# A new listed order of all steps in a fused attention and MLP kernel

## The chip, the cores and the metric

The kernel runs on one core of a Trainium2 chip. A core has five engines, each with an instruction stream of its own: TensorE (PE in the profile, with PEld for its weight loads), VectorE (DVE), ScalarE (ACT), GpSimd (POOL) and SyncE (SP), which here only starts DMA transfers. The metric is the device time of one execution in microseconds (us); lower is better.

## The reference

Two blocks follow each other. The first is a cross attention between 512 tokens and 32 states for each of 8 batches and 8 heads of width 64, in both directions. The second is an MLP on the 8 x (512 + 32) = 4352 rows that come out, with `d_model` 512 and `d_ff` 2048. All of it is float32; the two weights arrive as 64-bit floats.

```python
scores  = x @ state.T / 8;   a  = softmax(scores)    # (B, H, 512, 32)
xread   = a @ state
scores2 = state @ x.T / 8;   a2 = softmax(scores2)   # (B, H, 32, 512)
sread   = a2 @ x
rows    = concat(xread, sread)      # (B*544, H*64) after a transpose of heads
h       = rows @ w_in
out     = (h * erf(softplus(h))) @ w_out             # (4352, 512)
```

## The kernel before

**The order.** Every piece of work is a named step: `step(name, f)` (L248) stores a function, and nothing is issued when the steps are defined. At the end of the kernel (L1156 to L1164) a loop walks through `ORDER`, a list of 2532 names that fills lines 23 to 179, and issues each step in its turn through `issue` (L182). `in_order` (L1149) then fixes that every engine carries out its instructions in exactly this sequence. So each engine has a strict queue of its own, cut out of the one list: a step that has to wait holds up all that stands behind it on its engine, while the other engines go on until they need something from it. Semaphores for the data and for the reuse of buffers are put in by the framework from what each step reads and writes. Of the steps, 749 run on PE, 743 on DVE, 684 on ACT, 100 on POOL and 256 on SP.

```python
    for name in ORDER.split() or do:
        if name[0] == "~":
            k, n = name[1:].split("*")
            issue(name, lambda: warm(bank[int(k)][:, 0:P], int(n)))
        else:
            issue(name, do.pop(name) if ORDER.split() else do[name])
    in_order(begun)
```

A name such as `~7*3` is a filler: `warm` (L429) issues 3 products of the identity matrix into bank 7, which nobody reads. A float32 product shows up as two matmul instructions, a transpose as one.

**The start.** `load_x0` (steps `lx0` to `lx3`, L340) brings batch 0 of x, half of it on ACT's queue and half on SP's; `load_raw` (`i0l0`, `o0l0`, ...) brings the weights. `convert` (L375) turns 64-bit words into float32 in four steps: `a0` and `a1` on ACT, a shift `v0` on DVE (L383), and an integer add `v1` (L385), which for the first eight pieces (`i0` to `i3`, `o0` to `o3`, `BY_GPSIMD`, L20) runs on GpSimd and for the others on DVE. Piece `i0` comes in two parts (`i0...` and `i0+...`).

`attention0` (L433) handles batch 0. `x00` to `x31` turn x into banks (`xik`, with copies `xikc`; L444), `s0` turns the states (copies `s0c0`, `s0c1`, `s0c`), `t0` and `t1` are the token scores, `q0` and `q1` the state scores (copies `q0c`, `q1c`). For each half of the tokens, `max`, `less`, `exp`, `sum`, `inv` and `norm` make the softmax, `ta0` and `ta1` transpose it and `ta0c`, `ta1c` copy it to `y[0]`. The state softmax follows in `rest` (`big0`, `big1`, `big`, `wt`, `wz`, `wn`, transposes `tw0`, `tw1` with copies), then `read(0)` (L528): the product `rd0`, its copy `rn0`, a transpose `rt0`, a copy `rc0`. `ub` turns the states of batch 1.

`first_unit` (L967) is the MLP of batch 0. `n01`, `n00`, `n02`, `n10`, `n12` multiply states with parts of `w_in` (copies `...c0` on ACT and `...c1` on DVE), so that h can be had straight from the softmax; `h0L`, `h0R` to `h7L`, `h7R` (L987) are its half products, with a softplus `hks` (ACT), a copy `hkc` (DVE), an erf `hke` and a product `hkg`. The products with `w_out` are `o00` to `o36` (L1009), copied by `o0c` to `o3c` and stored by `o0d` to `o3d`.

**The units after it.** Batches 1 to 7 go through `attention(b)` (L554): loads `a1xq0` to `a1xq7` on SP, transposes `a1tx` on DVE, the scores `a1s` on PE, copies `a1c0`, `a1c1`, and two softmaxes. `load_st` (`lst1` to `lst8`, L363) brings their states on GpSimd's queue; `hold` is a one-column copy on GpSimd. Unit A1 to A7 is the first half of `d_ff` for a batch, SA and SB are the rows of the states, B0 to B7 the second half of `d_ff`. Within a unit, `mixed` (L646; `A1m`, `A1M1` to `A1M4`) multiplies states with `w_in`; `hidden` (L695, products L704) makes h with a scheme of seven products instead of eight block products, laid out by `chain` (L669): products `A1f01` to `A1f07` and `A1f11` to `A1f17` accumulate into three PSUM banks, with copies `c`, `u2`, `c11`, `u3`, `c21` (ACT) and adds `c22`, `c12` (DVE) between them, then softplus `s..`, erf `A1e0`, `A1e1` (L712) and products `A1g0`, `A1g1`. A copy from a bank to the next bank or to SBUF must be done before the next product may accumulate there.

`second_twice` and `inner` (L767 to L882) do the product with `w_out` by the same scheme at two levels, on products of 128 columns (L827): `A1ap10`, `A1ap11`, ... for the first four of the seven outer products, `A1bp...` for the other three, with copies `ac`, `au2`, `ac11`, `au3`, `ac21` (ACT) and adds `ac22`, `ac12` (DVE). `A1a2` to `A1a4` and `A1b2` to `A1b4` are sums of the left operands, `U2`, `U3`, `U4`, `C2`, `C12` sums of results in the buffer `res`, and `d0` to `d3`, `D0`, ... the stores (L735): plain ones on SP, accumulating ones on POOL. `res` is reused by the next unit, so `B2au2`, which writes it, waits for the store of unit B1 that reads the same part. In the second half of the kernel `second_last` (L884) is the last unit, B7, with adds `B7v..` and `B7C120`, `B7C121` and stores by halves, down to `B7d11`.

**Lists of weights.** `twice` (`t..`, `w..`) and `restore` prepare and take back the sums of `w_out` for the two-level scheme; `y11` to `y14` and the like (`sums_y`, L624) are sums of the softmax rows, kept in DRAM by `yk..`, `yl..` on SP until the second half loads them again (`yK..`, `yL..`).

Of the kernel before, what the change touches and what calls it, by code (L numbers as in the profile page):

```python
# [40 lines left out]
a3xq7 a2mx0 A1f1s12 o06 a3xq3 a2my0 a2sb0 A1e0 o14 a3xq1 a2x3 t32 A1e1 A1g0 t0k o16 a3xq6 A2m
a3xq5 A1g1 a2ex0 yk0 t1k o26 o0c t2k A2m11 a2x2 a2sm0 t4k A2m10 a2ey0 o30 a2iz a3tx0 a2x0 o1c
a2nm0 t6k A2m01 o2c a3tx2 o32 t3k a2ey1 A2m00 A2M1 a2ta0 o34 t42 y21 A2f01 a2ty0 a2ty1 o36 A2f0c
y22 a2kz A2M2 o2d t21 A2f06 y23 o3c t22 A2M3 A2f02 A2f0u2 A1q A2f05 A2f0c11 t23 A2f07 y24 A1A1
A1ap50 A2f0u3 A2f11 t44 a2z2 t12 o3d A2f0c22 A2f04 a2z1 t13 a2z0 A1ap10 A1A3 a2z3 A2f0c21 yk2
A2f1c A1ap11 yl2 A2M4 o0d A2f12 A1A2 A2f16 A2f0s22 T3 A2f03 A2f1u2 t62 A2f0s11 t5k A1ap51 t51 yk1
a2iy t02 A2f17 o1d t03 t33 t34 rd2 A2f1u3 A1A4 A1ac A2f14 rn20 t04 a3x0 rn21 A2f1c11 A2f0c12 rt2
A1ap20 A1a2 rc2 a3s A1b2 A1ap60 A1a3 a3c0 a4xq5 a3c1 A1ap61 a4xq6 t24 a3tu0 A1ap21 A1au2 a4xq3
A2f0s12 A2f15 t53 A1ac11 a4xq2 a3mx0 A1ap70 A2f0s21 a4xq1 A2f1c22 A1ap71 a3sb0 a3my0 a4xq0 A1bp10
A1au3 a3x3 A1ac22 A1bp11 A2f13 t14 t52 a3ey0 A1ap40 A1b4+ A1a4 a3ex0 A1ap41 t43 a3ey1 A1ap30 a3sm0  # L50
A1ac21 A1ap31 A1bc a3iz A2f1c21 A2f1c12 a3nm0 A1bp60 A1ac12 A1bp61 a4tx0 A1d0 A3m A2f1s12 a4xq7
A2f1s22 t54 A2f1s21 a3ta0 a4xq4 A1bu2 A1bp50 A3m00 A1b3 A2f1s11 A1bp51 A3m11 y31 A3f01 a3ty0 A3m01
A1bp20 A3m10 a3ty1 A1D0 A3f0c a3iy A1bp21 t63 a3kz A3M1 A1bp70 a3x2 t64 A1d2 y32 A1bp71 A2e0 A3M2
A3f05 A1b4 A3f06 A3M3 A1bu3 A3f02 y34 A3f0u2 y33 A1bc22 A2e1 A1bp40 a4tx2 A3f07 a3z3 A2g0 a3x1
A1bp41 A1bc11 a3z2 A1bp30 A3f0u3 a3z1 A3f0c11 a3z0 A3f04 A1bc21 A3f0c22 A3f11 A2g1 A3f0c21 A1bp31
A3f1c A2ap10 A3f16 A3M4 A3f12 A3f1u2 A1bc12 A2q A3f03 A1d1 A1d3 rd3 yl3 A3f0c12 A2A1 A3f17 rn30
a4x2 rn31 rt3 A2A3 A2ap50 rc3 A3f1u3 A3f15 A2A2 A3f14 A1D1 A3f1c22 A3f0s21 A2ap11 A3f0s11 A2A4 a4s
A2ac A2a2 A3f1s22 A2ap20 A3f1c21 a5xq1 A1U2 A3f1s12 A2ap60 A2a3 a5xq2 a4c1 A2ap61 a4c0 yk3 A1U3
a5xq3 A3f13 A2b2 A2au2 A1D4 A2ap21 A3f0s12 a4tu0 A3f1c11 A2ap70 a5xq7 A3f0s22 A2b4+ A2ac11 a4mx0
A2ap71 a5xq0 A3f1s11 A2ap51 A3f1c12 A2au3 a4sb0 a4my0 A2bp10 A3f1s21 A2bp11 A2ac22 A2ap40 a4x0  # L60
A1D2 A2a4 a4ex0 A2ap41 A1D3 A2b4 A2ap30 A2ac21 a4sm0 a5xq5 A2bc A2ap31 a4ey0 a4iz A2bp60 a4ey1
A2ac12 a4nm0 a5tx0 A2bp61 A4m A3e0 a4ta0 A2bp20 A4m11 A2b3 a4x1 A2bp21 A4m01 A2bp50 a4x3 a4ty0
A2bu2 A4m10 A2bp51 a4ty1 A4m00 A2bp70 y41 a4kz A3e1 A4M1 a5xq4 A2bp71 y43 A4f01 A4M3 a5xq6 A4M2
A4f05 A2bu3 A4f0c y42 A2d0 A2bp40 A2bc22 A2d2 A3g0 A4f06 A2bp41 A4f0u2 A4f02 A2bc11 a4iy a4z3 y44
A4f07 A3g1 a4z2 a4z0 A2bp30 A4f0u3 a4z1 A4f0c11 A2bp31 A2bc21 A4f04 A2D0 A4f0c22 A4f11 A2bc12
A4f0c21 A4M4 A2d1 A3ap10 A4f1c A3q A2d3 A4f03 a5tx2 A4f16 rd4 A2U2 A4f1u2 A3A1 A4f17 rn40 a5x0
rn41 A4f0c12 rt4 A3ap11 A2D1 A4f1u3 A3A2 rc4 A4f14 yl4 A3A3 A4f15 A4f0s22 A2U3 a5s A3a2 A2D2 A4f12
a5c0 a6xq0 A3A4 A3ac A3ap50 a5c1 a6xq2 A4f0s21 A3ap20 A4f1c22 A2D4 A3b2 A4f1c21 A3ap60 A4f1s22
a5tu0 A3ap61 A4f13 A3a3 A3au2 a6xq1 A4f0s12 A3ap21 a5mx0 A4f1c11 a5x1 A3ap70 A4f1s12 a6xq3 A3ac11
a5my0 a5sb0 A3ap71 a6xq7 A4f1c12 A3ap51 A3au3 A3bp10 A3ac22 A2D3 A3a4 A3ap40 a5ex0 A3bp11 A3b3  # L70
a5ey0 A3ap41 a6xq5 a5ey1 a5sm0 A3ap30 a6xq6 A3ac21 A3ap31 yk4 a5iz a5nm0 A5m A4f0s11 a6tx0 A3bc
A4f1s11 A3ac12 A3bp60 A5m01 a5ta0 A3d0 A5m10 A3bp61 A3d2 A5m11 A3bp20 a5ty0 A3bu2 A4f1s21 A3bp21
y51 a5ty1 A5m00 A3bp70 A5M1 a5kz A3bp71 a5iy A3d3 A5f01 y52 A5M3 A4e1 A3bp50 A3b4+ A3b4 A3D0
A3bp51 A5M2 A5f05 A3bu3 y53 A5f0c A3bc22 A3bp40 A4e0 y54 A4g1 A5f06 A3bp41 a5z0 A5f0u2 A5f02 a5x2
a5z1 A5M4 A5f07 a5z3 A5f0c11 A4g0 a5z2 A3bc11 A3bp30 a5x3 A5f0u3 A3bp31 a6xq4 A5f04 A5f0c22 A5f11
A3bc12 A5f0c21 A4q A5f03 A5f1c A3bc21 A4ap10 A3U2 A3d1 A5f16 yk5 A4A1 yl5 A5f12 A5f1u2 A5f0c12 rd5
A4A3 A5f17 rn51 a6tx2 rn50 A5f1c11 A4ap11 A5f1u3 A4A2 A3D1 rt5 A5f14 rc5 A4ac A3U3 a6s A4a2 A3D2
A5f15 a6c1 a7xq0 A4a3 a6c0 A4ap60 a7xq5 a6tu0 A4ap50 A5f1s11 A4ap61 A5f0s11 a6mx0 A4ap20 A4au2
A5f1c22 A5f0s12 a6sb0 A4ap21 a6my0 A5f1s22 a7xq4 A4ap70 A4ac11 A4ap51 A4A4 A3D4 A4ap71 a6ex0 A3D3
A4b2 A4bp10 A4au3 a6sm0 a6ey1 A4bp11 a7xq7 A5f13 a6ey0 a6iz A4ap40 A5f1c21 A5f1c12 a6nm0 A4ac22  # L80
A4ap41 A6m A5f0s21 A4ac21 A4a4 A4bc a6x2 A5f1s12 a6ta0 a7xq3 A4bp20 A6m00 A5f0s22 a7xq2 A4bp60
A4b3 A6m10 A6m11 A4bp61 a6ty1 A4ap30 A6m01 a7xq6 y61 A5f1s21 A6M1 A4ap31 A4bu2 a7xq1 a6ty0 A4bp21
# [1112 lines left out]
```

## Time and profile before

| what | value |
|---|---|
| median of three runs | 681.45 us (681.26, 681.45, 682.07) |
| span of the profiled execution | 680.2 us, 1.25 below the median |
| mean granted TensorE clock | 1.00 |
| instructions | 13851 |
| products of the two-level scheme (L827) | 47% of the chain that ended last |
| products of `hidden` (L704) | 27% of that chain |
| DMA | 87.15 MB, mean 128 GB/s |
| first x data lands | 4.19 us |
| PE never idle from / to | 36.36 / 676.4 us |
| last store lands | 678.91 us |

The span is the time from the first to the last recorded event of the profiled execution; the runs were timed without the profile. "Busy" is the time in which an engine had at least one instruction under way. The clock is the share of full speed that TensorE was granted. The chain that ended last is found by going back from the last instruction, at each step to what released it.

Starts of some steps in the profiled execution, in us: `t0` 8.34, `ta0` 15.12, `ta1` 17.34, `h1L` 17.83, `n02` 19.65, `n10` 23.41, `n12` 27.33, `rd0` 31.54, `a1s` 35.10, `A1m` 41.66, `A1f01` 48.79, `A1f06` 51.74. Twelve of the sixteen half products `h..` start before `a1s`.

### The profile page before, as it was taken

What the parts mean: (1) busy time and instruction counts of PE and PEld (TensorE: products, weight loads), DVE (VectorE), ACT (ScalarE), POOL (GpSimd) and SP (SyncE); (2) the same over time, 40 slices, a digit from 0 to 9 for tenths busy, and PEclk for the clock granted to TensorE, in tenths of its full rate; (3) what the DMA queues carried; (4) which work ended last, traced back from release to release, by engine and by line L of the source; (5) the groups of instructions that cost most, each with busy time, mean ns of one, the idle gap of its engine ahead of it and who ended that gap; (6) DMA issues with size and microseconds to landing.
All of it is one profiled execution on the core that took longest, in us unless ns stands there. A gap on an engine that the chain in (4) does not pass through costs nothing.

```text
span 680.2 us, 13851 instructions
## 1 busy us (share of the span) xinstructions
PE 673.4 (99%) x5584; PEld 590.2 (87%) x5584; DVE 581.1 (85%) x760; ACT 485.4 (71%) x759; POOL 130.9 (19%) x106
## 2 busy tenths in 40 slices
...
GB/s 299 219 249 118 198 219 98 163 163 191 159 185 158 145 173 123 156 139 136 224 271 212 58 63 115 72 61 57 32 83 34 44 29 116 19 67 18 46 89 121
DMA packets 145839, 87.15 MB, mean 128 GB/s; under 512 B 92784, under 2 KB 138096, under 8 KB 145776
## 3 DMA queue, kind: packets, MB, share of 16 engines
...
q10 hardware_dynamic: 544, 0.52, 0.2%
...
## 4 chain that ended last, share of the span: by engine, by line
PE 96%; DMA 1%; DVE 1%; SPq 1%; issue 0%; DVEq 0%
PE b L827 47%; PE b L704 27%; PE b L655 4%; PE b L1009 4%; PE b L1049 4%; PE b L757 4%; PE b L925 2%; PE b L987 1%; DMA big<-in_x_dram 1%; PE b L564 1%; PE b L539 1%; SPq L354 1%; PE b L456 1%; PE b L444 0%; DVE ring L244 0%; PE b L976 0%
## 5 line engine op out<-in xcount | busy, mean ns | idle before, releaser
L735 POOL DMA_DIRECT2D out_dram<-res x67 | 80.1, 1422 | 424.8 <-DVE res L242 205.9
L827 PEld LDWEIGHTS b<-big,ring 128*128 128x128 f32 x1196 | 145.4, 192 | 6.9 <-issue 1.7
L827 PE MATMUL b<-big,ring 128*128 128x128 f32 x1196 | 151.1, 275 | 0.0
L250 ACT COPY ring<-b 128x512 f32<-128x512 f32 (+1 forms) x136 | 78.4, 585 | 92.9 <-PE b L704 76.3
L704 PE MATMUL b<-y,m 128*128 128x256 f32 x480 | 121.3, 381 | 0.0
L250 ACT COPY res<-b 128x512 f32<-128x512 f32 (+2 forms) x126 | 64.6, 522 | 51.7 <-PE b L827 37.9
L704 PEld LDWEIGHTS b<-y,m 128*128 128x128 f32 x480 | 86.6, 190 | 12.3 <-issue 1.9
L704 PE MATMUL b<-sy,m 128*128 128x256 f32 x360 | 91.4, 381 | 0.0
L244 DVE TENSOR_TENSOR ring<-ring 128x2048 f32<-128x2048 f32 (+1 forms) x36 | 78.1, 2172 | 8.7 <-ACT ring L712 8.2
L693 ACT ACTIVATE ring<-ring 128x512 f32<-128x512 f32 x128 | 77.9, 632 | 2.5 <-DVE ring L242 2.0
L242 DVE TENSOR_TENSOR ring<-ring,b 128x512 f32<-128x512 f32 (+1 forms) x72 | 47.2, 658 | 31.3 <-PE b L704 15.2
L827 PEld LDWEIGHTS b<-ta,ring 128*128 128x128 f32 x548 | 67.7, 192 | 7.2 <-issue 3.4
L704 PEld LDWEIGHTS b<-sy,m 128*128 128x128 f32 x360 | 64.8, 190 | 10.0 <-issue 2.6
L827 PE MATMUL b<-ta,ring 128*128 128x128 f32 x548 | 72.4, 276 | 0.0
L243 DVE TENSOR_TENSOR ring<-ring 128x1024 f32<-128x1024 f32 (+3 forms) x66 | 70.7, 1080 | 0.1
L827 PE MATMUL b<-big,ta 128*128 128x128 f32 x572 | 70.7, 275 | 0.0
L827 PEld LDWEIGHTS b<-big,ta 128*128 128x128 f32 x572 | 67.8, 192 | 1.3 <-ACT b L250 0.8
L242 DVE TENSOR_TENSOR res<-res,b 128x512 f32<-128x512 f32 (+2 forms) x60 | 36.2, 604 | 27.4 <-PE b L827 15.6
L712 ACT ACTIVATE ring<-ring 128x2048 f32<-128x2048 f32 x30 | 57.2, 1913 | 0.2
L250 ACT COPY b<-b 128x512 f32<-128x512 f32 (+2 forms) x63 | 34.3, 547 | 16.1 <-PE b L704 8.2
L242 DVE TENSOR_TENSOR res<-res 128x512 f32<-128x512 f32 (+1 forms) x56 | 42.1, 753 | 2.3 <-ACT res L250 1.3
L242 DVE TENSOR_TENSOR ring<-ring 128x1024 f32<-128x1024 f32 (+1 forms) x35 | 39.8, 1143 | 0.3
...
## 6 DMA issues: line engine op xcount, KB each, us to landing
...
```

The source lines that it names most:

```text
L242: add = lambda o, a, b: tt(o, a, b, op=ALU.add)
L243: sub = lambda o, a, b: tt(o, a, b, op=ALU.subtract)
L244: mul = lambda o, a, b: tt(o, a, b, op=ALU.mult)
L250: do[name] = lambda: f(*args)
L655: pe.matmul(out=to[j][e][q, :], lhsT=by, rhs=w_in[r, 4 * j:4 * j + 4, i, :], start=True, stop=True)
L693: act.activation(out=o, in_=i, func=ACTF.Softplus)
L704: pe.matmul(out=to[:, i], lhsT=xs[n - 1][:, q:q + P], rhs=ys[n - 1], start=(start and i == 0), stop=(i == 1), skip_group_check=True)
L712: step(u + "e%d" % o, lambda s=s: act.activation(out=s, in_=s, func=ACTF.Erf))
L735: nc.gpsimd.dma_start(out=to, in_=of, accum_op=ALU.add)
L757: pe.matmul(out=to[:, E2 * h:E2 * h + E2], lhsT=a[:, k // 2, k % 2], rhs=rhs[n][:, k], start=(start and h == 0 and k == 0), stop=(k == 3), ...
L827: pe.matmul(out=out_[:, P * j:P * j + P], lhsT=lhs[:, i], rhs=rhs[:, i], start=(start and j == 0 and i == 0), stop=(i == 1), skip_group_ch ...
L1009: pe.matmul(out=bank[3 + r % 3], lhsT=s[:, k, P * r:P * r + P], rhs=wo[0].w[:, k, :], start=(k == 0), stop=(k == NT - 1))
```

## The change

Only the list `ORDER` is different. The new list has the same 2532 names, the three fillers `~7*3`, `~7*1` and `~7*5` included, each once; no step's function, buffer or engine is touched, and what depends on what stays the same. The order of all steps is another, from the first line to the last. In the start, for example:

- `~7*3` stands ahead of `x30` (before: behind `exp1`), `~7*1` behind `x20`, and `x20`, `x00` ahead of `x10`;
- `q0` and `q1` stand ahead of `t1`;
- `h1L` stands ahead of `ta1`, and `n02` ahead of `ta1` and `h0L`;
- `i0v1` stands ahead of `i0+v1`, `norm1` behind `i1v1`, `o0a1` behind `h1s`, `h0s` and `n12c0`;
- the loads `lst1` to `lst8` are spread over the start (before: all behind `hold`);
- more of the products `o..` stand ahead of `A1f06`.

Later, `B1C2` and `B2au2` stand nearer to each other, and in the last unit `B7D0` stands ahead of the stores of `B6`, and the adds `B7v..` and `B7C120`, `B7C121` have another sequence on DVE; PE's last steps keep theirs. The diff has 155 lines on each side; the places named here are these:

```diff
@@ -21,161 +21,161 @@
-warm lx3 own lx2 lst0 lx1 lx0 i0l0 i0l1 i1l0 i1l1 i2l1 x30 s0 x30c x10 s0c0 s0c1 x31 x10c x20 x00
-x20c x11 i2l0 x00c x21 x01 i0a0 t0 i3l1 i0a1 i0v0 x11c x01c x21c x31c i0+a0 s0c i3l0 t1 i0+a1 max0
-i0+v0 less0 ls1 i0+v1 q0 exp0 max1 i1a0 i0v1 q1 sum0 less1 o0l0 inv0 exp1 ~7*3 n01 norm0 a1xq4 n00
-n01c0 sum1 n00c0 q1c ~7*1 ta0 o0l1 i1a1 inv1 a1xq5 i1v0 norm1 ta0c i1v1 n01c1 i2a0 q0c ~7*5 ta1
-n00c1 big0 h1L i2a1 big1 h0L ta1c a1xq2 i2v0 i3a0 n02 big i2v1 ub o1l1 n02c1 h1R wt0 ubc h0R n02c0
-a1xq1 i3a1 h3L i3v0 a1xq6 wt1 n10 h0c i3v1 o0a0 h2L n10c1 h1c a1xq7 h3R n10c0 a1tx2 o0a1 o1l0 h5L
-a1xq0 wz y01 n12 wn1 h2R a1xq3 n12c1 h1s wn0 tw1 o3l1 n12c0 y02 h3s o3l0 h2c tw0 h0s o2l0 h3c tw1c
-h6L y04 tw0c o0v0 h2s yl0 rd0 a1tx3 o0v1 a1tx0 h6R a1x3 rn0 h0e a1tx1 o2l1 rt0 h5R h6c a1x2 rc0
-o1a0 h0g a1s h2e h5c h4L o1v0 a1c0 h7L o1a1 h2g h7R a2xq3 a1c1 a1tu0 o1v1 h4R h7c a2xq6 o00 a1tu1
-h5s a1my0 h7s hold a1mx0 h4s a2xq7 A1m h6s lst3 a1mx1 lst2 a1sb0 lst4 a1sb1 a2xq1 a1ex0 o02 lst1
-a1my1 a1ex1 lst5 a1sm0 A1m11 lst7 a1sm1 A1m10 o20 lst6 a1ey0 a1iz A1M1 lst8 A1m01 a1nm0 a1ey1 o22
-a2xq2 a1nm1 A1m00 a1ta0 a1ta1 a1x0 A1f01 a2xq4 y11 h4e a1ty0 A1f05 a1iy a1ty1 A1f0c u1 y12 o3a0
-a1kz A1f02 A1M2 a2xq5 h4c o2a0 A1f06 A1M3 a2xq0 o10 y13 A1f0c11 A1M4 A1f0u2 y14 h6e a1x1 o3v0
-A1f07 o2v0 o2a1 u0 T1 A1f0u3 A1f11 o3a1 a1z3 o2v1 A1f0c22 A1f04 a1z2 a2tx2 a1z0 a1z1 A1f03 A1f0c21
...
-B3f0c11 B3f05 B3f04 B3f0c22 B3f0s11 B1C2 B3f11 B2ac B3f03 B3f0s22 B2A2 B1d3 B3f0c21 B2ap50 B3f0s12
-B1d2 B2A3 B2ap20 B3f1c B3f0c12 B3f12 B2A4 B3f16 B3f1c11 B3f15 B2a2 B3f1u2 B2ap21 B2b2 B3f17 B2a4
-B2ap60 B3f1u3 B2a3 B2ap51 B2ac11 B3f14 B3f1c22 B3f0s21 B1C12 B2ap61 B2b4 B1d1 B3f13 B2au2 yL4
-B3f1c21 B2bp10 B3f1c12 yK5 B2bp11 B2ap70 B3e0 B2ap71 B4m B2au3 B2ac22 B3g0 B2ap40 B3f1s11 B4m10
...
-B7au2 B7ap51 B6U3 B7ap70 B6U4 B6C2 B7ap71 B7ap20 B7au3 B6d3 B7ac22 B7ap21 B6d2 B7A2 B7ap30 B7ac11
-B6C12 B7ap31 B7A4 B7ap40 B7ac12 B7ap41 B7A3 B7p30 B7ac21 B7pc0 B7D0 B7q- B7pc1 B7p60 B6d1 B7w3
-B7w5 B7w4 B7p61 B7pu20 B7p70 B7pu21 B7w2 B7D1 B7C120 B7p71 B7v20 B7d10 B7d20 B7p31 B7v21 B7v31
-B7v30 B7d31 B7d30 B7d21 B7C121 B7d11
+lx3 lx2 warm own lst0 lx0 lx1 i0l0 ~7*3 i0l1 i1l0 i1l1 i2l1 x30 x30c s0 x20 ~7*1 s0c1 x00 x20c
+i2l0 s0c0 x10 x00c x21 x31 x10c x01 i3l1 x11 x31c t0 x01c s0c x11c i0a0 x21c i0v0 i0a1 i3l0 q0
+max0 i0+a0 q1 i0v1 less0 t1 i0+a1 ls1 i0+v0 exp0 q1c i0+v1 sum0 ~7*5 o0l0 i1a0 max1 a1xq4 inv0
+lst2 n00 i1a1 less1 o0l1 norm0 n01 exp1 i1v0 ta0 a1xq5 n00c0 n01c1 n01c0 q0c i1v1 ta0c sum1 i2a0
+h1L n00c1 inv1 i2a1 norm1 a1xq2 n02 i2v0 ta1 n02c0 h0L big0 i2v1 ta1c big1 i3a0 ub o1l1 h1R big
+n02c1 ubc i3a1 lst6 n10 h1c h0R wt0 y01 a1xq1 i3v0 h3L n10c0 wt1 n10c1 a1xq6 y02 h5L o0a0 i3v1 wz
+a1xq7 h3R o0v0 h2L o1l0 h1s n12 wn0 a1xq0 h0s h5R wn1 a1tx2 n12c0 o0a1 a1xq3 tw0 n12c1 y04 tw1 h0c
+h3s o3l1 h2R o0v1 a1tx3 tw1c h7L tw0c h5c o3l0 h2s h2c rd0 o2l0 lst1 h3c yl0 lst3 h4L t01 a1x3 rn0
+h0e a1tx1 lst8 o2l1 rt0 h7R a1tx0 lst7 rc0 h2e h0g a1s o1a0 h6L h2g a1x2 h4R a1c0 a2xq3 o1v0 a1c1
+hold o00 h7c lst4 a1tu0 lst5 h4c h7s h6R a1tu1 h4s A1m h5s a1mx1 a2xq6 o1a1 a1mx0 a1sb1 h6s a1my0
+o20 a1sb0 a2xq7 h6c o1v1 a1ex1 o10 a1my1 a2xq1 a1ex0 a1sm1 A1m01 a1sm0 a2xq2 o12 a1ey1 a1iz a1ey0
+a1nm0 a1x0 A1m00 a1nm1 u1 A1m11 a2xq4 o22 a1ta0 A1m10 a1ta1 a1ty1 A1f01 a1ty0 h4e o02 y11 a1kz
+A1M1 A1f0c a2xq5 o3a0 y12 A1M2 u0 y13 a2xq0 o2a0 A1f06 y14 A1M3 A1f02 A1f0u2 a1x1 a1iy y03 o2a1
+a1z3 o2v0 A1f07 T1 A1f05 A1f0u3 A1f0c11 A1M4 A1f04 a1z2 o3a1 a1z0 A1f0c22 o2v1 A1f11 a1z1 a2tx2
...
+B2ap11 B2a2 B3f04 B2ac B1U3 B3f11 B3f0c21 B1U4 B2ap50 B3f1c B1C2 B3f16 B1C12 B2ap20 B3f1u2 B1d2
+B3f17 B2ap60 B3f1u3 B1d3 B3f0s12 B3f1c22 B3f14 B1d1 B3f13 yL4 B3f1c21 B2ap61 B3f1c12 B2A4 B2ap21
+B2ap51 B2a3 B2au2 B4m B2ac11 B2a4 B2A3 B2ap70 B2ap71 B2b2 B3f12 B2au3 B2ac22 B2bp10 yK5 B4m01
...
+B7ap21 B7ac22 B6C12 B7ap30 B7ac11 B7A3 B7ap31 B6C2 B7ap40 B7ap41 B7ac12 B7p30 B7ac21 B7pc1 B7w3
+B7pc0 B7D0 B7q- B7p60 B7w5 B6d3 B7w4 B7p61 B7pu20 B6d1 B7p70 B7pu21 B6d2 B7w2 B7p71 B7v30 B7v20
+B7D1 B7d30 B7d20 B7p31 B7v21 B7v31 B7d21 B7C120 B7d31 B7d10 B7C121 B7d11
```

More of the change, by code (lines that the diff above doesn't have):

```diff
@@ L41 @@
[L41 to L82, printed above, removed]
@@ new lines @@
+a6xq3 A3bp60 A5M1 y54 A5f02 A3b3 A3d0 A4e1 a6xq0 A3bp50 A5M2 A5M3 a5x0 A3bp61 a5z3 y53 A5f06 A3bu2
+a5z2 A4g1 A4e0 A3d3 A3D0 A3bp70 A5f05 a6xq2 A5f0u2 A3b4 A3bp71 A5f0c11 A3bp51 A5M4 A3bc11 A5f07
+a5z1 a6tx2 A3bu3 a5z0 A3bp40 A3d2 A5f0u3 A3bc22 A5f04 A5f0c22 A4g0 A5f11 A5f0c21 A3bp41 A5f1c
+A3bp30 A3bc21 A3b4+ A5f03 A4q A5f16 A5f0s22 A5f0c12 A3bp31 A4A1 A5f1u2 rd5 A5f0s11 A3bc12 A4ap10
+rn51 a6tx0 A3d1 rn50 A5f0s12 rt5 a6x0 A5f17 rc5 yk4 A3U2 a6s A4A2 A5f1u3 A5f15 A3U3 A3D1 a7xq1
+a6c0 A4ap50 A4A3 a6c1 A4ap51 a7xq4 A5f1c22 A5f14 a6tu0 A4ap11 A5f1c21 a6x2 a6mx0 A5f13 yl5 A4ac
@@ new lines @@
+A4bu3 A5g1 A6f07 A4d0 A4d3 A4bp40 yl6 A6f0u3 A6f11 A6f0c22 A4bp41 A4bc22 A4D0 A6f04 a7tx2 A6f03
+A6f0c21 A5q A6f1c A4bp30 A6f0c12 rd6 a7tx0 A4bp31 rn61 A6f16 A4bc21 A4bc12 rn60 A4bc11 A5A1 rt6
+A6f15 A4d1 rc6 A6f1u2 A4d2 A5ap10 A4U2 A5A3 a7s A6f0s12 A5A2 A6f12 A4D1 a7c1 A6f17 a7c0 A5ap11
+a7tu0 A6f1u3 A6f14 A5ac A6f1c22 A6f1c11 A5ap20 a7mx0 A6f1s22 A6f1s11 A5ap21 A5a2 A6f1c21 A6f13
+A6f0s11 A4U3 A5ap60 a7my0 a7sb0 A5ap61 A6f1c12 a7ey0 A5ap50 A5a3 A4D3 a7ex0 A7m A5au2 A5a4 A4D2
+A5ac11 a7ey1 a7sm0 A5ap70 A7m11 A5ap51 A5A4 A5ap71 a7iz A5bp10 a7nm0 A5au3 A5ac22 A5ap40 A5b2
```

214 lines of the change are left out of this document (123 added, 91 removed).

## The prediction

> **What bounds the kernel now.** I read the page's first and fourth part, then the busy time by stretches, then the first 70 us of the timeline engine by engine. TensorE is the bound:
>
> ```profile
> span 680.2 us, 13851 instructions
> ...
> PE 673.4 (99%) x5584; PEld 590.2 (87%) x5584; DVE 581.1 (85%) x760; ACT 485.4 (71%) x759; POOL 130.9 (19%) x106
> ...
> PE 96%; DMA 1%; DVE 1%; SPq 1%; issue 0%; DVEq 0%
> ```
>
> Busy time by stretches (us, then each engine's busy time) tells where the missing per cent lies:
>
> ```profile
> 0.00:20.00 20.00, 17.87 (x218) 15.47 (x218) 12.02 (x27) 13.02 (x22) 6.43 (x10) 1.00 0.98 305
> 20.00:36.36 16.36, 15.48 (x186) 10.04 (x170) 13.55 (x27) 15.07 (x23) 7.22 (x3) 1.00 0.91 212
> 36.36:68.00 31.64, 31.64 (x217) 20.15 (x217) 31.12 (x53) 28.45 (x46) 12.49 (x12) 1.00 0.73 173
> 68.00:300.00 232.00, 232.00 (x2076) 196.96 (x2075) 221.89 (x285) 177.85 (x286) 52.95 (x37) 1.00 0.75 164
> 300.00:641.00 341.00, 341.00 (x2640) 313.90 (x2640) 275.34 (x338) 238.72 (x366) 44.56 (x38) 1.00 0.42 89
> ```
>
> From 36.36 us on PE is never idle. A busy PE could still be slow, so I took start-to-start times: 128-column products follow each other every 111.7 ns, 256-column ones every 216 ns, over the whole body. Beyond these pitches I find, after 40 us, only the fixed steps around the 64-row products (L655, L564, L539), and 0.06, 0.03 and 0.02 us at three places. **So nothing is to be won after 40 us; there a new order can only lose.** Before it, the same sum gives 6.9 us of PE waits in 0 to 40 us; 18 filler products (L431, 111 ns each when warm, 2.0 us) lie there as well. Some of the waits:
>
> ```profile
> 6.35 2.16 PE L444 MATMUL b<-ident,big 128*128 128x128 f32 x14 [0.82 <-DMA big<-in_x_dram]
> 17.34 0.66 PE L469 MATMUL b<-ident,ring 128*128 128x128 f32 x4 [0.46 <-DVE ring L244]
> 26.27 1.13 PE L987 MATMUL b<-y,m 128*128 128x256 f32 x4 [0.27 <-ACT m L250]
> 30.48 1.13 PE L987 MATMUL b<-y,m 128*128 128x256 f32 x4 [0.33 <-ACT ring L693]
> ```
>
> The ceiling of the gain is therefore about 6.9 us, 1%. The tail, 676.4 to 680.2, is a last add and a store that lands 2.1 us after issue.
>
> **The change, part by part.** Both lists hold the same 2532 names, fillers included, so no instruction is added or removed and every dependency runs between the same steps. Only places change.
>
> *1. Opening.* Six of the fillers (`~7*3`) now stand before the first turn, `x30`. Warm-up products run at 213 ns, `x30` began at 4.33, straight after them. Six more cost 0.67 (at 111 ns) to 1.28 us (at 213): I take 0.9, x30 at 5.2 to 5.3. Against it, `x20` and `x00`, whose data landed at 4.62 and 5.58, now come ahead of `x10`, which waited until 6.35 for data landing at 6.30. Walking on (turns 0.22 each, s0 0.55, copies 0.37 to 0.41): `x01` waits for `x00c`, done 7.5, and `t0` starts at 8.0 instead of 8.34. Gain 0.35 (0.05 to 0.4).
>
> *2. Softmax of token 0.* `q0`, `q1` (1.37 together) now stand ahead of `t1`, so `t1` ends at 13.1 instead of 12.0. VectorE has `max1` ahead of `inv0`, so `inv0` waits for it: max1 13.1 to 13.8, inv0 to 14.2, less1 to 14.9, norm0 to 15.5 (now 15.05). Loss 0.45 at `ta0`. But `h1L` needs only `ta0c`, not `ta1` as the present order makes it wait: ta0 15.6, ta0c 16.25 to 16.85, h1L 16.9 against 17.83. Gain 0.9.
>
> *3. GpSimd's adds (`i1v1`, `i2v1`, `i3v1`).* i1v0 ends at 16.1 instead of 16.69, so i1v1 (2.41 alone; 2.71 now, because norm1 was in its way) ends near 18.6, and `n02` starts there instead of 19.65. PE stands still from 17.8 to 18.6 and shortly before `n10`. Here the shared port counts:
>
> ```profile
> 20.25 2.41 POOL L385 TENSOR_TENSOR w_in<-w_in,ring 128x1024 uint32<-128x1024 uint32 x1 [0.69 <-DVE m L510]
> ...
> 21.02 2.19 DVE L383 TENSOR_SCALAR w_in<-w_in 128x1024 uint32<-128x1024 uint32 x1
> ```
>
> The shift i3v0 takes 0.69 elsewhere (L383 at 30.91) and 2.19 when it meets a GpSimd add: it ends 0.55 after the add. In the new order norm1 falls into i1v1 (starts near 18.6, ta1 near 19.4), and o0v0 into i3v1; i3v0 no longer meets one. With that, n12 comes at 26.8 instead of 27.33, after the same eight half products.
>
> *4. To the second attention (`a1s`).* `o0a1` is now behind h1s and h0s on ScalarE, so the softplus table (1.28) is loaded at 26.0 instead of 27.3, and h7L runs at 30.0 with no wait. rd0 waits 0.65 for tw0c (31.4), rt0 0.15, a1s 0.5 for a1tx0 (34.8). At a1s's end the new order has done one half product (0.86) more and is 0.2 earlier: **gain 1.05**. It lasts only if the next chain allows it: in the trace A1M2 ended 0.07 us ahead of A1f06. In the new list two more `o` products stand ahead of A1f06, and VectorE's listed work grows by less, which leaves 1.4 us more there. So I carry 1.05.
>
> *5. Queues.* SP's first 46 entries are the same in both lists. The eight `lst` loads on POOL (0.6 to 0.7 each) move between the adds, where POOL idles or i3v0 comes later: 0. Loads of x then stand at least 7.8 us of PE work ahead of use (5.7 now). Stores before a reuse of `res` get shorter: from `B1C2` to `B2au2` 8.0 us instead of 8.7 to 9.8; C2 itself is 1.2, landing took 6.2 to 6.9 after it. That can be late by 0 to 0.9 once; `B2ap70` then waits. I take 0.1.
>
> *6. Body: cover of the copies.* Products that accumulate onto a copied bank wait for: product, ScalarE copy, next product. An example (A5f17, its copy, A5f14):
>
> ```profile
> 214.12 1.21 ACT L250 COPY ring<-b 128x512 f32<-128x512 f32 x2
> 214.33 1.08 PEld L827 LDWEIGHTS b<-ta,ring 128*128 128x128 f32 x8
> 214.54 1.05 PE L827 MATMUL b<-ta,ring 128*128 128x128 f32 x8
> ...
> 215.54 0.60 PE L704 MATMUL b<-sy,m 128*128 128x256 f32 x2
> ```
>
> Other products cover 214.54 to 215.54, 1.00; the copy ended at 215.33, 0.21 before. So 0.79 is needed. After 40 us the present list has one 512-wide copy covered by 0.86 to 0.89 (four 256-column or eight 128-column products), the new list 33. Each has 0.07 to 0.10 in hand, if ScalarE is free. The three places of the trace with 0.05 in hand lost 0.02 to 0.06. Bounds: 0 to 33 x 0.06 = 2.0; I take 0.2, since most are above 0.05.
>
> *7. ScalarE's tables.* Counting changes between softplus, erf and exp along ScalarE's list: 58 stretches now, 53 then, 5 x 1.28 = 6.4 us less on an engine that is 71% busy. Nothing on the path; it favours step 6.
>
> *8. Tail.* PE's last steps keep their order. `B7D0` now precedes three stores on POOL (1.2 to 1.7 each, from 666.9: until 672.7); `B7D1` waits for D0's landing (672.7) as now and would land near 677.4, 1.5 ahead of the last store's 678.9. 0.
>
> Sum: -1.05 + 0.1 + 0.2 = -0.75. The span of 680.2 becomes 679.45. The median of the runs, 681.45, is 1.25 above the span, which I leave: **680.7 us**. About 0.2% (1.36 us) is what a measurement tells from no change.
>
> **A rule against it.** In the trace inv0's first part (L426, 13.86, 0.17) began while GpSimd's add i0v1 (12.71 to 14.01) still ran, and took no longer than its twin at 15.68. The Trainium skill, "SBUF — State Buffer", § Who interferes with whom, says that a VectorE instruction in a 2-port mode, tensor_scalar among them, is fully blocked while GpSimd holds the pair. The row at 13.86 speaks weakly against it for tiny ones, i3v0 for it.
>
> **Rivals.**
> - *Tiny steps lock too.* If inv1, big and wz wait for the running add, inv1 starts 0.8 later, ta1 at 19.75, big holds n02c1 back to 23.0, i3v0 slides to 24.6 and n12 to 28.4; rn0 comes at 35.6 and a1s at 37.0, one half product ahead, so 1.05 behind in all: 681.45 + 1.05 + 0.3 = 682.8. For it: i3v0. Against: inv0. 0.12, half of it over the bound.
> - *ScalarE is late at the thin covers* (slower). A softplus (0.63) or an erf (1.91) stands directly ahead of many of the 33 copies. If they run on 0.2 late on average, each place loses 0.1 to 0.15: 33 x 0.12 = 4.0, so 681.45 - 1.05 + 4.0 = 684.4. It decides from 0.073 a place on (2.4 in all). For it: margins that the present order does not take. Against: the present order hit 0.05 to 0.2 at some fifteen places and lost 0.1 in all. 0.26.
> - *The start gains more*: rd0 and a1s without waits (1.15 more), no loss in the body: 679.25 to 679.8. 0.20. For it: 6.9 us of waits are there. Against: landings and GpSimd's adds pace the start, and stay.
> - *The list does not do what it says*, later landings hurt: only the `B1` stores have less lead. Inside the forecast.
>
> **Numbers.** Forecast case (680.7, own range 679.9 to 682.0) 0.42. Faster by over 0.2% (below 680.09): 0.20 + 0.07 of the forecast case = 0.27. Slower (above 682.81): 0.06 + 0.25 = 0.31. Within: 0.42. Range 679.3 to 684.6: it takes in the higher start gain and the late ScalarE.
>
> **What would show it.** Step 1: t0 near 8.0; step 2: h1L near 16.9; step 3: n02 near 18.65, n10 near 22.4, n12 near 26.8; step 4: a1s near 34.9 with 13 half products before it (12 now). Step 6: PE's pitch broken by under 0.1 us at the copies; step 7: some 56 table loads (61 now). I am wrong if PE's idle time after 40 us passes 1 us, or if n12 starts after 28.

## The result and the profile after

The changed kernel takes 690.95 us (690.30 to 692.18, 4 runs) against 681.76 us (681.26 to 682.25, 4 runs): 1.37% slower, ratio 1.0137 with a 95% interval of 1.0122 to 1.0151. The forecast was 680.7 us, in a range of 679.3 to 684.6. The profiled execution has a span of 689.6 us, 9.4 more than before. In one execution of e7 below (1162.82 us) the granted clock was 0.557; it is left out of e7's time.

From the page of the changed kernel: the span, the busy times, and the chain that ended last by engines.

```profile
span 689.6 us, 13834 instructions
...
PE 678.6 (98%) x5584; PEld 591.6 (86%) x5584; DVE 591.1 (86%) x760; ACT 474.8 (69%) x751; POOL 134.5 (20%) x106
...
PE 85%; DVE 9%; ACT 2%; DMA 2%; issue 1%; POOL 0%; SPq 0%; ACTq 0%; DVEq 0%; POOLq 0%
```

Three things are to be seen. The chain went through PE for 96% of the span and now does for 85%; 9% of it is VectorE. PE carries out the same 5584 matmul instructions and is "busy" for 5.2 us more: a busy PE was slower, so its busy time hides more than half of the loss. And VectorE is busy for 10 us more with the same 760 instructions: some of them last longer.

Busy time by stretches of the changed kernel (us, then PE, PEld, DVE, ACT, POOL, clock, DMA share, GB/s):

```profile
36.36:68.00 31.64, 29.49 (x203) 17.66 (x202) 31.36 (x47) 27.34 (x39) 8.47 (x6) 1.00 0.77 199
68.00:300.00 232.00, 231.25 (x2010) 193.69 (x1998) 223.56 (x285) 175.11 (x285) 53.98 (x35) 1.00 0.71 156
300.00:641.00 341.00, 340.86 (x2685) 312.19 (x2685) 275.48 (x339) 225.39 (x358) 46.78 (x40) 1.00 0.44 91
```

Between 36 and 68 us PE now stands still for 2.15 us, while VectorE is full (31.36 us; it was nearly so before, with 31.12). Behind that PE looks as unbroken as before. So I added up what busy time can't show: for each PE step, the time from its first product to the first product of the next step, less its products at their fixed pitch. This lost time, by stages:

| lost PE time, us | before | after | more |
|---|---|---|---|
| 0 to 40 us | 6.10 | 6.49 | 0.39 |
| 40 to 80 us | 0.98 | 4.01 | 3.03 |
| from 80 us to the last product | 4.75 | 9.43 | 4.68 |
| from the last PE step's start to the last landing | 4.43 | 5.70 | 1.27 |
| sum | | | 9.37 |

The sum is the difference of the spans. Of the first row some 0.5 us are chance: the six fillers `~7*3` ahead of `x30` took 1.26 us in this execution, all at 213 ns, but 0.77 us in the traces of e2 and e8 and 0.67 us in that of e4, which have the same opening (there they follow each other every 112 ns, from the first or the second on). Without that the first row would be near zero. Each of the other stages has a cause of its own.

**VectorE held by GpSimd (0 to 80 us).** The timeline of the changed kernel, VectorE (start, duration, line, operation, tiles):

```profile
17.34 0.68 DVE L495 TENSOR_REDUCE z<-ring 128x16 f32<-128x512 f32 x1
17.94 0.28 DVE L250 COPY m<-b 128x128 f32<-128x128 f32 x1
18.13 1.07 DVE L426 TENSOR_SCALAR z<-z 128x16 f32<-128x16 f32 x1
...
22.05 1.35 DVE L510 TENSOR_SCALAR m<-m 128x2 f32<-128x2 f32 x1
...
25.71 2.56 DVE L243 TENSOR_TENSOR sy<-y,sy 128x256 f32<-128x256 f32 x1
...
44.03 2.29 DVE L587 TENSOR_TENSOR big<-big,m 128x512 f32<-128x512 f32 x1
...
58.64 2.90 DVE L243 TENSOR_TENSOR m<-m 128x512 f32<-128x512 f32 x1
61.46 0.68 DVE L242 TENSOR_TENSOR ring<-ring,b 128x512 f32<-128x512 f32 x1
```

and GpSimd in the same time:

```profile
16.78 2.39 POOL L385 TENSOR_TENSOR w_in<-w_in,big 128x1024 uint32<-128x1024 uint32 x1 [2.37 <-ACT m L250]
20.96 2.41 POOL L385 TENSOR_TENSOR w_in<-w_in,ring 128x1024 uint32<-128x1024 uint32 x1 [1.79 <-DVE w_in L383]
...
25.59 2.39 POOL L385 TENSOR_TENSOR w_in<-w_in,ring 128x1024 uint32<-128x1024 uint32 x1 [1.70 <-DMA big<-in_moe_w_out_dram]
...
43.26 2.51 POOL L385 TENSOR_TENSOR ta<-ta,big 128x1024 uint32<-128x1024 uint32 x1 [2.94 <-ACT big L381]
58.20 2.78 POOL L385 TENSOR_TENSOR ta<-ta,ring 128x1024 uint32<-128x1024 uint32 x1 [12.43 <-DMA big<-in_x_dram]
```

The same operations in the old kernel (the fourth line is `a1sb0` and `a1sb1` together):

```profile
15.68 0.17 DVE L426 TENSOR_SCALAR z<-z 128x16 f32<-128x16 f32 x1
...
20.04 0.15 DVE L510 TENSOR_SCALAR m<-m 128x2 f32<-128x2 f32 x1
...
28.86 0.42 DVE L243 TENSOR_TENSOR sy<-y,sy 128x256 f32<-128x256 f32 x1
...
42.17 1.29 DVE L587 TENSOR_TENSOR big<-big,m 128x512 f32<-128x512 f32 x2
...
53.12 0.68 DVE L243 TENSOR_TENSOR m<-m 128x512 f32<-128x512 f32 x1
```

Take the first add: 16.78 + 2.39 = 19.17. The reduce at 17.34 and the copy out of PSUM (`b`) at 17.94 run in their usual time under it. `inv1` on 16 columns at 18.13 lasts 1.07 instead of 0.17 and ends at 19.20, 0.03 after the add. It is the same with `big` (ends 0.03 after the add), `y02` (0.28), `a1sb0` and `A1M4` (0.55). VectorE is held for 0.90 + 1.20 + 2.15 + 1.61 + 2.22 = 8.1 us in all. The profile shows it as duration, not as a wait. In the old kernel the same comparison gives 1.7 us, nearly all of it at `i3v0`: there, reads of PSUM, transposes and reduces stand under the adds.

Not every hold reaches PE. `inv1` holds `norm1` back, for which `ta1` waits 0.46; `big` holds `ubc` back, for which `n10` waits 0.55 in its middle; later PE waits 0.86 us for `A1M2` ahead of `A1f06`, 1.46 us for `A1f0c22` ahead of `A1f03` and 0.41 ahead of `A1f16`. The 2.15 us of `y02` cost it nothing: from 24.6 to 54 us PE has no wait above 0.2 us.

**Thin covers (from 80 us).** One of the 33 places, `B0f06`, which accumulates onto the bank that `B0f0c` copies:

```profile
377.32 1.03 PE L704 MATMUL b<-y,m 128*128 128x256 f32 x4
...
378.18 2.01 PE L704 MATMUL b<-sy,m 128*128 128x256 f32 x8
...
378.44 0.57 ACT L250 COPY b<-b 128x512 f32<-128x512 f32 x1 [1.16 <-PE b L704]
...
379.06 0.73 PEld L704 LDWEIGHTS b<-sy,m 128*128 128x128 f32 x4 [0.25 <-ACT b L250]
...
380.03 0.81 PE L757 MATMUL b<-ta,ring 128*128 128x256 f32 x3
```

ScalarE had been idle (1.16) and starts the copy 0.47 after the last product's start; the copy ends at 379.01. `B0f05` covers 378.18 to 379.05, so `B0f06` starts only 0.01 late, at 379.06. But its weights are loaded only then (PEld idle for 0.25, ended by ACT), and the next step comes at 380.03, 0.97 after it instead of 0.86. That the late weight load is what costs the 0.10 is read from these rows; no run separates it. The place costs 0.12. The same sums over all products that wait for a copy give a rule of this trace: a copy that ends 0.15 us or more ahead costs nothing, one that ends d us ahead costs about 0.155 - d in the product's own run, at most 0.10, plus the lateness. By kind of copy and cover: `c` 0.117 (cover 0.86) and 0.087 (0.89), `u2` 0.103, `u3` 0.049, `ac` 0.115, `au2` and `au3` 0.047; copies of 384 columns 0 to 0.08. After 80 us 41 such places cost 3.1 us; 13 more, where ScalarE or VectorE itself was late, 2.2 us (0.7 of it where `A3f01` waits for `a3ta0`, behind an `L426` held for 1.7 us). The old kernel loses 0.3 in this way.

**The tail.** The issues of the end of the run, from 664 us on (queue, count, KB each, median us from issue to landing), before and then after:

```profile
out_dram<-ring SPq DMA_DIRECT2D x6, 128.0 KB, 2.2
out_dram<-ring POOLq DMA_DIRECT2D x2, 256.0 KB, 5.1
out_dram<-res POOLq DMA_DIRECT2D x1, 256.0 KB, 6.4
```

```profile
out_dram<-res POOLq DMA_DIRECT2D x4, 256.0 KB, 6.5
out_dram<-ring SPq DMA_DIRECT2D x6, 128.0 KB, 4.0
out_dram<-ring POOLq DMA_DIRECT2D x2, 256.0 KB, 5.6
```

`B6`'s three accumulating stores now stand behind `B7D0` and land at 681.8 to 684.8, with `B7D1` at 686.6; the last six stores run among them and take 4.0 us instead of 2.2.

### The profile page after: what moved, and what is told of

Read it like the earlier page. It is cut to its first block, busy times and chain, and to the rows that moved or that the text cites. A ratio compares the mean times of both kernels' runs of the same rounds, so it can differ in the third digit from the quotient of the medians.

```text
span 689.6 us, 13834 instructions
## 1 busy us (share of the span) xinstructions
PE 678.6 (98%) x5584; PEld 591.6 (86%) x5584; DVE 591.1 (86%) x760; ACT 474.8 (69%) x751; POOL 134.5 (20%) x106
## 4 chain that ended last, share of the span: by engine, by line
PE 85%; DVE 9%; ACT 2%; DMA 2%; issue 1%; POOL 0%; SPq 0%; ACTq 0%; DVEq 0%; POOLq 0%
PE b L827 42%; PE b L704 24%; PE b L1049 4%; PE b L757 4%; PE b L655 3%; PE b L1009 3%; PE b L925 2%; DMA out_dram<-res 1%; DVE res L242 1%; PE b L539 1%; DVE big L250 1%; PE b L431 1%; PE b L564 1%; PE b L987 1%; DVE m L243 1%; DVE ring L243 1%
## 5 line engine op out<-in xcount | busy, mean ns | idle before, releaser
L827 PE MATMUL b<-big,ring 128*128 128x128 f32 x1196 | 155.2, 276 | 0.0
L827 PEld LDWEIGHTS b<-big,ring 128*128 128x128 f32 x1196 | 147.7, 192 | 6.9 <-issue 3.4
L704 PE MATMUL b<-sy,m 128*128 128x256 f32 x360 | 93.2, 385 | 0.8 <-DVE m L243 0.7
L827 PE MATMUL b<-big,ta 128*128 128x128 f32 x572 | 72.8, 276 | 0.0
L704 PEld LDWEIGHTS b<-sy,m 128*128 128x128 f32 x360 | 63.4, 190 | 10.5 <-ACT b L250 2.1
L242 DVE TENSOR_TENSOR res<-res 128x512 f32<-128x512 f32 (+1 forms) x56 | 45.5, 815 | 1.7 <-ACT res L250 0.6
```

What stands on the lines that cost most here:

```text
L242: add = lambda o, a, b: tt(o, a, b, op=ALU.add)
L704: pe.matmul(out=to[:, i], lhsT=xs[n - 1][:, q:q + P], rhs=ys[n - 1], start=(start and i == 0), stop=(i == 1), skip_group_check=True)
L827: pe.matmul(out=out_[:, P * j:P * j + P], lhsT=lhs[:, i], rhs=rhs[:, i], start=(start and j == 0 and i == 0), stop=(i == 1), skip_group_ch ...
```

## Experiments

All times are medians, beside 681.6 to 682.0 us of the old kernel on the same chip. e1, e2, e8 and e9 join two lists: down to a step the one, then the other without what is already issued.

**e1: old start, new body.**

```diff
-(new list)
+(old list down to A2m, then the new list)
```

> The old list down to A2m, the new list for all that remains. Theory (the loss has separate places: 3.4 us before 80 us, 4.7 us of broken PE pitch after it, 1.3 us in the tail): the 3.4 us go, 690.95 - 3.4 = 687.6 us. Rival (the losses after 80 us are the start's lateness carried on by VectorE and ScalarE): with the old start most of them go too, 682 to 684 us.

Measured: 692.48 us, 1.0162 (1.0131 to 1.0194). Neither forecast came true. The trace shows why: down to 80 us the old start's loss is back (6.83 us instead of 10.50), but the two lists don't fit at the joint, where PE loses 5.5 us. It waits 3.73 for `a2ta0` ahead of `A2f01`; and then, from 88.88 to 92.50 us, the granted clock is 0.53: the products of `A2f01` follow each other every 0.427 us instead of 0.216 and those of `o36` every 0.854 instead of 0.429, which is 1.77 more. Behind it the losses are those of the new list (1.75 us at 120 to 160, the new kernel 1.79), so they don't come from the start; `B4ap70` waited another 1.04 for `B4au2`. The parts of the loss are seen in the trace as the theory has them; the time as a whole tells nothing.

**e2: new start, old body.**

```diff
-(old list)
+(new list down to A2m, then the old list)
```

> The new list down to A2m, the old list for all that remains. Theory: only the start's loss is left, 681.76 + 3.4 = 685.2 us. Rival (lateness is carried on): 688 us or more, with PE waits after 80 us.

Measured: 685.93 us, 1.0067 (1.0050 to 1.0084); span 683.6, 3.4 above the old one. From 80 us on it loses 5.1 us, the old kernel 4.75. So the start alone costs 3.4 us by the spans and 4.2 by the medians, and its lateness isn't carried on: theory's 685.2 is near, and the rival's 688 is not reached.

**e3: covers widened.**

```diff
-B0A1 B1f1c B1f16 w62 w03 B0ap10
+B0A1 B1f1c B0ap10 B1f16 w62 w03
```

and so on, 30 steps. In this kernel `A1bp51` stands ahead of `A1bp50`, which clears the bank, so a part of unit A1's sums is lost.

> The new list with 30 PE steps moved by a few places, so that 35 of the 41 copies covered by 0.86 to 0.89 us after 80 us get 1.0 us or more; no other engine's order is touched. Theory (a copy that ends less than 0.155 us ahead of the product that waits for it breaks the pitch, by up to 0.10 us beside the wait itself): these 35 places lost 2.7 us in the new kernel's trace, so 688.2 us. Rival (ScalarE comes late whatever the cover is): the copies end later with respect to PE by other work, under 1 us is won, 690 us or more.

Measured: 694.57 us, 1.0190 (1.0175 to 1.0205), slower than the changed kernel. At the 35 places the loss fell from 2.7 to 0.9 us (0.7 of that at `B3ap70`). But the moved products now wait themselves: 1.18 at `B4ap70`, 0.59 at `B0f05`, 0.55 at `A2f16`, 0.53 at `A3f06`, 0.47 at `B6ap70` and less elsewhere, and the start came 0.5 later (`A2m` at 80.49 instead of 79.98; `t0` is late by as much, with the same list, because the products ran at 213 ns for longer). Inconclusive as a time; e6 asks the same question the other way round.

**e4: old tail.**

```diff
-(new list)
+(new list down to B7ap51, then the old list)
```

> The new list down to B7ap51, the old list for the last 14 us: the stores of unit B6 go out ahead of B7D0, as before. Theory (those stores share the DMA engines with the last ones): from the last product's end to the last landing 2.5 us instead of 3.8, so 689.7 us. Rival (the tail is only shifted): 690.95 us, the last store lands 3.3 us after its add again.

Measured: 689.33 us, 1.0116 (1.0101 to 1.0131). From the issues of its last 23 us:

```profile
out_dram<-res POOLq DMA_DIRECT2D x3, 256.0 KB, 5.5
out_dram<-ring SPq DMA_DIRECT2D x6, 128.0 KB, 2.2
```

The last six stores take 2.2 us again, and from the last PE step to the last landing it is 4.50 us (old 4.43, new 5.70). The old order of the last 14 us, some steps on VectorE and ScalarE included, takes the loss away, as the theory has it. That the stores hinder each other on the DMA engines was not measured by itself.

**e5: one pair exchanged on VectorE.**

```diff
-o2v0 A1f07 T1 A1f05 A1f0u3 A1f0c11 A1M4 A1f04
+o2v0 A1f07 A1M4 A1f05 A1f0u3 A1f0c11 T1 A1f04
```

> The new list with T1 and A1M4 exchanged, one pair on VectorE. Theory (a VectorE operation on two SBUF operands that falls due while a GpSimd add runs waits for the add's end; A1M4 does so for 2.2 us at 58.6): A1M4 now starts ahead of the add o2v1, ends after 0.7 us, and PE's waits before A1f03 and A1f16 (1.9 us) go: 689 us. Rival (VectorE is simply full, the wait only moves to T1 or c22): under 0.5 us is won, 690.5 us or more.

Measured: 689.32 us, 1.0106 (1.0086 to 1.0126), 1.6 less than the changed kernel. VectorE in e5:

```profile
57.53 0.68 DVE L243 TENSOR_TENSOR m<-m 128x512 f32<-128x512 f32 x1
58.13 1.22 DVE L243 TENSOR_TENSOR ta<-ta 128x1024 f32<-128x1024 f32 x1
59.27 0.68 DVE L242 TENSOR_TENSOR ring<-ring,b 128x512 f32<-128x512 f32 x1
```

and GpSimd:

```profile
58.23 3.40 POOL L385 TENSOR_TENSOR ta<-ta,ring 128x1024 uint32<-128x1024 uint32 x1 [12.42 <-DVE m L243]
```

`A1M4` takes 0.68 instead of 2.90. `T1`, which started 0.10 ahead of the add, is not held; now the add is, 3.40 instead of 2.4 to 2.8. Whoever comes first holds the other. The waits of 1.46 and 0.41 us ahead of `A1f03` and `A1f16` are gone, the one for `A1M2` (0.86) stays. The theory holds.

**e6: thin covers put into the old list.**

```diff
-A2bp40 A2bc22 A2d2 A3g0 A4f06 A2bp41
+A4f06 A2bp40 A2bc22 A2d2 A3g0 A2bp41
```

and so on at 24 places.

> The old list with 24 PE steps put one place earlier, so that 24 copies of 512 columns are covered by 0.86 to 0.89 us instead of 1.34 to 1.79; ScalarE's and VectorE's order is the old one. Theory (such a cover always costs, 0.05 to 0.13 us by the kind of copy as read in the new kernel's trace): 24 places, 2.3 us together, 684.1 us. Rival (only a late ScalarE makes a thin cover dear, and here it comes in time): 681.75 us.

Measured: 686.45 us, 1.0060 (1.0043 to 1.0077), 4.9 more instead of 2.3. Both forecasts of the time missed, and each named a part of the loss. Two of the 24 covers came out wide, since later moves lay beside them. At 18 places ScalarE started the copy 0.42 or 0.47 (0.36 for `au2`) after the last product: the loss is 1.87 us, 1.80 by the kinds listed above. At four it came late; one of them is `B6f16`:

```profile
593.95 0.59 ACT L250 COPY ring<-b 128x512 f32<-128x512 f32 x1 [0.69 <-PE b L704]
...
594.57 0.57 ACT L250 COPY b<-b 128x512 f32<-128x512 f32 x1
...
595.19 0.73 PEld L704 LDWEIGHTS b<-sy,m 128*128 128x128 f32 x4 [0.63 <-ACT b L250]
595.19 1.13 PE L704 MATMUL b<-sy,m 128*128 128x256 f32 x4 [0.44 <-ACT b L250]
```

The copy needed (594.57) stands right behind another one (593.95), so it starts 1.09 after its product instead of 0.47, and PE waits 0.60 and then loses the 0.10 as well. The four cost 2.5 us. So a thin cover costs its 0.05 to 0.13 us even where ScalarE comes in time, which the rival denied, and a late ScalarE costs more, which the theory left out. In the old kernel these covers are 1.34 us or wider, and none of this is seen.

**e7: VectorE mended at four places.**

```diff
-big0 big1 big n02c1 ubc h1c y01 ... n10c1 y02 wz ... n12c1 y04 h0c
+big0 big1 n02c1 ubc h1c big y01 ... n10c1 h0c wz ... n12c1 y02 y04
-a1my0 a1sb0 h6c a1my1 ... T1 ... A1M4
+a1my0 h6c a1my1 a1sb0 ... A1M4 ... T1
```

(VectorE's steps alone, `...` for steps left as they are.)

> The new list with VectorE's order mended at four places: big behind n02c1, ubc and h1c; h0c ahead of y02 and y02 behind n12c1; h6c and a1my1 ahead of a1sb0; T1 and A1M4 exchanged. Theory (VectorE is held for 8 us in all by GpSimd's adds, 7 of them at these places, and PE's 3.4 us of more waits before 80 us come from that): 3.4 us less or a little better, 687.5 us. Rival (the GpSimd adds themselves, or the order of PE, make the start late): 689 us, as with one pair.

Measured: 1.0088 (1.0063 to 1.0113), at 686.8, 688.9 and 689.1 us. These times reach from below the theory's number to the rival's and decide nothing; e8 and e9 carry the weight.

**e8: the mended start, old body.**

```diff
-(e7's list)
+(e7's list down to A2m, then the old list)
```

> The mended start of the run before this one down to A2m, then the old list. Theory: the start then costs no more than the old one, and nothing else is left of the change: 681.8 us, between 680.5 and 682.5. Rival: 683.5 us or more.

Measured: 682.20 us, 1.0005 (0.9994 to 1.0016), against 685.93 in e2, which differs in VectorE's order at these places alone. Span 680.1. Its busy time from 36 us on:

```profile
36.36:68.00 31.64, 31.64 (x221) 19.72 (x214) 31.15 (x52) 29.96 (x47) 10.02 (x6) 1.00 0.85 211
```

PE is unbroken again. `big` takes 0.16, `y02` 0.41, `A1M4` 0.68; `inv1` is still held (1.07), and `wz` now is (1.58 instead of 0.13), `a1sb0` a little (1.10 instead of 0.68); PE does not wait for `wz` or `a1sb0`. The theory holds: PE's order is that of e2, and moving VectorE's steps at four places, mostly out from under the adds, takes away the whole cost of the start. That the new sequence also serves PE better by itself is not excluded; the durations here and e5 say that the holds are the larger part. What it does not bring is a gain: `A2m` starts at 76.07, 0.49 ahead of the old kernel, and the last PE step at 674.40 (old 674.48).

**e9: start, tail and ten covers mended.**

```diff
-B2U3 B4f17 B2U4 B3ap11 B2C2
+B2U3 B3ap11 B4f17 B2U4 B2C2
```

for example; beside it e7's places and e4's tail.

> The new list with three things mended at once: VectorE's order at the four places of the start, the old order in the last 14 us, and 10 of the thin covers widened to 1.34 us or more by moving one PE step each ahead of the waiting product. Theory (the losses add): 690.95 - 3.4 - 1.4 - 0.8 = 685.3 us; what is left over the old list are some 25 thin covers (2.2 us) and products for which ScalarE or VectorE is late (1.9 us). Rival (PE, once it is ahead, meets other waits): 687 us or more.

Measured: 686.18 us, 1.0065 (1.0051 to 1.0079): 4.8 us of the 9.2 are gone, 5.6 were expected: about halfway between theory and rival. The losses add for the most part. 31 thin covers are left with 1.9 us, and 14 late products with 3.2 us; `B6a3` holds `B6ap70` for 0.5 us in the mended list.

**e10 to e12: can the old start be bettered?** Three old lists with other steps in the first 45 us.

```diff
-x30 s0 x30c x10 s0c0 s0c1 x31 x10c x20 x00
+x30 s0 x20 x00 s0c0 x20c x00c x30c x10
-i3v1 o0a0 h2L n10c1 h1c a1xq7 h3R n10c0
+i3v1 n10c0 o0a0 h2L n10c1 h1c a1xq7 h3R
```

> The old list with a few moves in the first 36 us: x20 and x00 ahead of x10, without fillers ahead of them; n10c0 ahead of o0a0, o0a1 behind tw0c on ScalarE; a1xq0 and a1xq3 ahead of o1l0 on SP, rn0 ahead of a1tx0 on VectorE. Theory (PE's waits for lx1, n10c0, h0s, tw0c and rn0, 2.4 us in the old trace, are due to these places): t0 at 7.6 instead of 8.3, h5L 0.4 earlier, 1.0 us in all, 680.6 us. Rival (VectorE's chain from a1s to A1M2, which ended 0.07 us ahead of A1f06, takes it back): 681.4 us.

> The run before this one with o10 ahead of A1f06, so that PE has 1.9 us more of work before it needs A1M2. If VectorE's chain takes the gain back at A1f06, this gives it again: 680.6 us where the run before has 681.4. If not, both are alike.

> The run with the old list and a new start (the tenth), and in it rc0 ahead of h0e, a1c0 and a1c1 ahead of o1a0 on ScalarE, a1tu0 and a1tu1 ahead of o1v0 on VectorE. In the tenth run a1s stood for 1.4 us in its middle, since its second bank is freed by rc0, which was behind an erf with its table load. Theory: that wait goes and VectorE's chain to A1M2 starts 1 us earlier: 680.7 us. Rival (ScalarE's time is only moved; h0e and the softplus steps come later and A1m waits for them): 682.3 us or more.

Measured: e10 682.32 us, 1.0010 (1.0001 to 1.0019); e11 683.99 us, 1.0034 (1.0022 to 1.0047); e12 682.67 us, 1.0011 (1.0002 to 1.0020). None is faster; e10 and e11 missed what was forecast for them, e12 came out as its rival had it. In e10 `n10c0`, `h0s` and `rn0` no longer hold PE, `rd0` comes at 30.67 (31.54 before), and `a1s` begins at 33.74, but in its middle it waits 1.5 us for `rc0`. In e11 `o10` delays the chain of copies behind `A1f06` (0.89 us at `A1f07`). In e12 that wait is gone, `a1s` ends at 34.79 instead of 36.36, and 1.6 us less are lost down to 40 us; then `o02` waits 1.11 for `o1v1` and `A1f01` 1.02 for `a1ta0`, and at 347 us another 0.95 is lost for `A7bc`. So in e12 the work of the other engines between `a1s` and `A1f01` sets the time, and what PE gained before it is given back. No version of this study is faster than the old one.

## Why the prediction was wrong, step by step

- **Step 1, opening:** not refuted. `x30` came at 5.59, not 5.2 to 5.3, and `t0` at 8.59, not 8.0: the six fillers cost 1.26, the 213 ns end of the bounds. But the same opening gives `x30` at 4.69 and `t0` at 7.84 in e4, and 5.10 and 8.10 in e2 and e8. How long the products run at 213 ns differs from execution to execution, and the forecast lies inside that spread.
- **Step 2, softmax:** the order of events was right. `t1` ended at 13.79 instead of 13.1, and everything behind it followed: `h1L` at 17.41 instead of 16.9. Most of that is the opening's 0.6; in e2, with the fast fillers, `h1L` came at 16.93.
- **Step 3, GpSimd's adds:** here the prediction failed first. It took a hold for the shift `i3v0` alone and none for the tiny steps. In the trace `inv1` and `big` were held (2.1 us), `y02` too, and `n12` came at 29.08 instead of 26.8. Of these 2.3 us 0.6 came with the opening, 0.4 up to `n10` (`ta1` waits 0.46 behind `inv1`'s hold) and 0.55 behind `big`'s. The rest is a slip in the sum: behind `n10` (0.59) stand five half products of 0.86 in the new list, 4.9 us of PE work where the prediction allowed 4.4; in e8, without the wait behind `big`, it is 5.11. The row that was weighed against the rule, `inv0` at 13.86, ended at 14.03; the add ended at 14.01. It was consistent with a hold all along: so close to the add's end it could show no more than 0.15 us. That was too weak a row to price a rival at 0.12.
- **Step 4, to `a1s`:** 36.40 with 13 half products instead of 34.9: a loss of 1.30 - 0.86 = 0.44 in place of a gain of 1.05. The waits of 1.3 us expected ahead of `rd0`, `rt0` and `a1s` did not come: from `n12` to `a1s` it is 7.32 us instead of 8.1. That this hides part of step 3's error is luck. "1.4 us more" of room ahead of `A1f06` was counted in VectorE's listed work, without holds: `a1sb0` and `A1M4` lost 3.8 us more there, and PE waited from 51 to 64 us. The rival "tiny steps lock too" had the right mechanism and only a quarter of the holds (2.1 of 8.1 us): it went through the tiny steps and not through all operations on two SBUF operands.
- **Step 5, queues:** the late store exists, at `B4au2` and not at `B2au2`. It costs little in the changed kernel's trace, as forecast, but 0.2 to 1.2 us in e1, e3, e4, e5 and e9, in e1 and e3 more than the 0.9 that the step allowed.
- **Step 6, covers:** the mechanism was in the sum and the size was off by more than ten. 0.79 us was read as enough, with "0.07 to 0.10 in hand". What is needed is about 0.95 to 1.0, since a copy must end 0.155 us ahead. I had looked at the start of the waiting product (0.02 to 0.06 late) and not at the 0.10 that it loses in its own run. The old trace had such a row: `A6bp10` began 0.06 late and took 0.10 more than its pitch. 0.2 us were forecast; 3.1 us were lost at thin covers and 1.9 us more than before at products for which an engine was late (0.3 us of these 5.0 are fixed steps ahead of 64-row products, which the old list loses elsewhere; hence 4.7). The rival "ScalarE is late at the thin covers" named the second part, at 4.0 us.
- **Step 7, tables:** right. 53 table loads instead of 61, and nothing on the path: ScalarE is busy for 10.6 us less, and the kernel is slower.
- **Step 8, tail:** wrong. It asked whether `B7D1` lands in time, which it does, and not what `B6`'s stores do to those beside them: 1.27 us.
- **The signs of being wrong** both came: `n12` started after 28, and PE's idle time after 40 us passed 1 us (2.15 us between 36 and 68 us).
- **The ceiling** ("there a new order can only lose", after 40 us) was right, and so was the sign that should have followed from it: with at most 6.9 us to win in the start and 640 us of unbroken pitch to lose, 0.31 for slower was too little.

The Trainium skill, "SBUF — State Buffer", § Who interferes with whom, also says that a VectorE instruction with two SBUF inputs contends with a GpSimd instruction that reads SBUF, and that the one that starts first holds the pair for its whole run. The traces agree: `y02`, `a1sb0` and `A1M4` end 0.28 to 0.55 after the add, and in e5 the add is the one that lasts 3.40. The prediction cited the 2-port half of that section, to which the tensor_scalar steps `inv1` and `big` belong, and passed over this one.

What stays open: the lateness of ScalarE and VectorE at 13 places after 80 us (2.2 us) was read from the trace and not undone by a run, except in part by e2; and e7 by itself. Some 0.8 us of what e9 was expected to win back did not come.
